# A gated MLP kernel: w_out in float16 parts, and transposes by VectorE and DRAM in place of TensorE's

## The chip, the cores and the metric

The kernel runs on one core of one Trainium2 chip. A core has five engines, each with its own instruction queue and strict order: TensorE (PE; its weight loads are shown apart as PEld), VectorE (DVE), ScalarE (ACT), GpSimd (POOL) and SyncE (SP), which here issues nearly all DMAs. The metric is the device time of one execution in microseconds (us).

## The reference

x has 2048 rows of 512. A softmax attention with 32 heads of 16 comes first, then a gated MLP whose gate mixes rows:

```
h  = x + attention(LN(x) @ wqkv) @ wo
z  = gelu(LN(h) @ w_in)               # 2048 x 1376
z1, z2 = z[:, :688], LN(z[:, 688:])
g  = w_sp @ z2 + b_sp                 # w_sp is 2048 x 2048
h2 = h + (z1 * g) @ w_out             # w_out is 688 x 512
```

Both LN are without weights. All is float32.

## The kernel before

Matrix products with near-float32 results are made of two float16 parts (high and low, the low part being the rest after the high): `mm3` issues three matmuls for one (high x high, high x low, low x high; lines 108 to 110), and `split` makes the parts (99 the high part on ACT, 105 the low one on VectorE). The program has these stages, on one core:

- **Up to about 165 us:** LN(x) and the projection to q, k, v.
- **To about 1295 us: attention.** PE, VectorE and ACT are nearly full; POOL works through a list of chores with durations that a planner spreads over the loop, among them the scaling and splitting of w_sp, w_in, wo, and of w_out in six pieces (`out_piece`), which go to DRAM as float32-like pairs (`wu_scr`).
- **1296 to 1455 us, "the middle".** Sixteen blocks of 128 rows in the order 0, 1, 8, 9, 2, 10, 3, 11, ..., 7, 15. Step k works on several blocks at once: 12 matmuls of width 512 make h of block k+2 (`make_h`, L743) from o's parts (`split_o`, ACT's high part L735 and VectorE's low part L736), VectorE adds x (L747) and takes the statistics, nb (L764) is the LN's shift, ACT normalises to hn (L1274). `turn` transposes hn on PE in four 128x128 steps (L1191), and `split` makes hT's parts. z of block k comes in four groups of 12 matmuls (`make_z`), the right half first; ACT takes the gelu (L1206). VectorE's statistics zst (L1268) and zmv (L1219) of z's right half lead to another nb (L764, also a helper's line, now from zmv); ACT normalises z (L1222); z's left half goes to DRAM (`z_scr`).
- From k with a partner (rows 8 on), `gate_z` makes the parts of the gate's seven products from both blocks' z: b22, b21, b11 and t1, t2, t3, n4 (a scheme with seven products in place of eight). `parts` writes the high part (L1210) on ACT or POOL and the low one (L1211) on POOL or VectorE. `meanwhile` asks for the next operand block of w_sp, multiplies o by its factors on POOL (L730), and asks for o, rc and xr of a block further on (L722, L725, L728 on SP).
- **1456 to 1731 us, "the end".** Eight pairs p of row blocks (p, p+8). A pair is seven products (`product`, 24 matmuls of width 344 each) into PSUM tiles A, B, C; between them ACT and VectorE build pr = z1 * g for both blocks (p1 L1397, q5, v; VectorE's L1412, L1416, L1420, L1426). `Out` transposes pr on PE in float32 (six steps of 128, L1327), splits it into fp32r parts, multiplies by w_out's pairs `wu` in 17 matmuls of 512 (mm3, L1352, L1353), and adds h (L1357). The transposes and the output of one pair stand between the products of the next.

`manual_schedule` means that in the middle and the end each engine's order is the order in which the code is written. Tiles live in pools; the pools of the middle are released as wholes, and the first DMAs into the end's tiles wait for that.

Of the kernel before, what the change touches and what calls it, by code (L numbers as in the profile page):

```python
# [40 lines left out]
FB = [(i * P, min(P, FH - i * P)) for i in range(6)]  # L41
# [18 lines left out]
def block_kernel(ctx: ExitStack, tc: tile.TileContext, x, wqkv, wo, w_in, w_sp4, b_sp, w_out, out):  # L60
# [30 lines left out]
    wu_scr = [dram.tile([P, 2, D], F32, name=f"wu{i}_scr") for i in range(len(FB))]  # L91
# [625 lines left out]
    def load_o(sb):  # L717

        c = slice(sb * P, (sb + 1) * P)
        o = e2.tile([P, DB, P], F32, name="o")  # L720
        for d in range(DB):
            nc.sync.dma_start(o[:, d, :], o_scr[d, :, :DH, c])  # L722
        rc = e2.tile([P, DB, P], F32, name="rc")
        for d in range(DB):
            nc.sync.dma_start(rc[:, d, :], r_scr[8 * d:8 * d + 8, c].rearrange(  # L725
                "h (o s) -> h o s", o=1).to_broadcast([8, DH, P]))
# [5 lines left out]
    def split_o(sb):  # L732
        o = os_.pop(sb)
        o2s[sb] = [e2.tile([P, DB, P], F16, name=f"o2{i}", bufs=1) for i in range(2)]
        nc.scalar.activation(o2s[sb][0], o, AF.Copy, scale=o_up)  # L735
# [48 lines left out]
    with ExitStack() as at:  # L784
# [181 lines left out]
        def out_piece(i):  # L966

            f0, n = FB[i]
            got, load = piece(w_out[f0:f0 + n, :], n)
            t = []  # L970

            def high():
                t.append(wp.tile([P, 2, D], F32R, name="wup", bufs=4)[:n])
                pool.tensor_copy(t[0][:, 0], got[0])

            def low():
                pool.tensor_sub(t[0][:, 1], got[0], t[0][:, 0].bitcast(F32))

            job(load, [(lambda: times(got[0], out_down), TS), (high, CAST), (low, TT)], 12)
            soon(len(chores) + LATER, lambda: nc.sync.dma_start(wu_scr[i][:n], t[0].bitcast(F32)))  # L980

# [69 lines left out]
        for i in range(len(FB)):  # L1051
            out_piece(i)
# [6 lines left out]
        for n in range(0, len(units), 2):  # L1059
# [86 lines left out]
            if n in (476, 480, 504, 508):  # L1146
                asked.append(load_o(h_rows[{476: 0, 480: 1, 504: 2, 508: 3}[n]]))
            if n in (484, 488, 508):
                asked.pop(0)()
            if n in (488, 500, 510):  # L1150
                split_o(h_rows[(n - 488) // 11])
# [28 lines left out]
    with ExitStack() as mid:  # L1180
# [13 lines left out]

        def new_z(sb):
# [13 lines left out]
        def parts(name, k, src, eh, el):  # L1209
            (nc.gpsimd.tensor_copy if eh == "pool" else nc.scalar.copy)(T[name][0][:, k, :], src)  # L1210
            (nc.gpsimd if el == "pool" else nc.vector).tensor_sub(T[name][1][:, k, :], src, T[name][0][:, k, :])  # L1211

        def gate_z(sb, meanwhile):
# [30 lines left out]
            e.tensor_sub(t2, b21, t2)  # L1244
            parts("n4", k, t2, eh, el)

        row = dict(enumerate(h_rows))
        with tc.manual_schedule(engines={E.PE, E.Activation, E.DVE, E.Pool, E.SP}):
# [3 lines left out]
            for k in range(NB):  # L1252
# [4 lines left out]
                if k + 3 < NB:  # L1257
                    split_o(row[k + 3])
                if new is not None:
                    mv, rs = scale_h(new)  # L1260
                    nb = minus_mean(e2, mv, rs)
                new_z(sb)
                make_z(sb, 1, 0)
                if k + 1 < NB:
                    turn(row[k + 1])
                make_z(sb, 1, 1)
                for c in range(2):
                    nc.vector.bn_stats(zst[sb][:, c, :], zs[sb][1][:, c * FC:(c + 1) * FC])  # L1268
                make_z(sb, 0, 0)
                make_z(sb, 0, 1)  # L1270
                hTs.pop(sb)
                if new is not None:
                    hns[new] = e2.tile([P, D], F32, name="hn", bufs=3)
                    nc.scalar.activation(hns[new], xrs.pop(new), AF.Identity, bias=nb, scale=rs)  # L1274
# [5 lines left out]
                def meanwhile():  # L1280
                    if k + 4 < NB:
                        asked.pop(0)()
                    if k + 5 < NB:
                        asked.append(load_o(row[k + 5]))
# [6 lines left out]
    with ExitStack() as fin:  # L1291
# [4 lines left out]
        ps_g = fin.enter_context(tc.tile_pool(name="fin_g", bufs=4, space=PSUM))  # L1296
        WB = len(FB) - 1
        TW = P // 2
        fn = FB[-1][1]
# [9 lines left out]
        class Out:  # L1309


            def __init__(self, tb, h, pr):
                self.rows, self.h, self.pr = slice(tb * P, (tb + 1) * P), h, pr
                self.pT = self.acc = None

            def turn(self, *halves):

                if self.pT is None:
                    self.pT = [f2.tile([P, WB + 1, P], F32R, name="pT0"),
                               f2.tile([P, WB, P], F32R, name="pT1")]  # L1320
                    self.tps = {}
                for half in halves:
                    i0 = 3 * half
                    tp = self.tps[half] = ps_t.tile([P, 4, P], F32, name="tp")
                    for i in range(i0, i0 + 3):
                        c = i * P if i < WB else FH - TW
                        nc.tensor.transpose(tp[:, i - i0, :], self.pr[:, c:c + P], ident)  # L1327

            def split(self, *halves):

                hi, lo = self.pT
                for half in halves:
                    i0, tp = 3 * half, self.tps.pop(half)
                    n = 3 - half
                    nc.scalar.activation(hi[:, i0:i0 + 3, :], tp[:, :3, :], AF.Copy)  # L1335
                    nc.vector.tensor_sub(lo[:, i0:i0 + n, :], tp[:, :n, :], hi[:, i0:i0 + n, :].bitcast(F32))
                    if half:
                        t = hi[TW:, WB, :]
# [127 lines left out]
```

## Time and profile before

| | us |
|---|---|
| median of 3 executions (1732.65 to 1733.68) | 1732.87 |
| the profiled execution | 1732.66 |
| its span, first to last instruction | 1730.9 |
| PE busy / DVE / ACT / POOL | 1713.6 / 1389.4 / 1301.3 / 824.8 |
| granted TensorE clock | 1.000 |

A row of the time line reads: start, duration, engine, line, operation, output <- input, shape, and in brackets how long the engine stood idle before it and what released it. A row of a group reads: line, engine, operation, names, count | busy us, mean ns | idle us before them and the releasers. A row of a table by windows reads: from:to, length, busy us of PE, PEld, DVE, ACT, POOL with their instruction counts, granted clock, share of the DMA engines, GB/s. A matmul's end in the profile is modelled, so the pace of matmuls is read from their starts.

### The profile page before, as it was taken

How to read it: one execution, taken by the hardware profiler on the slowest of the kernel's cores; microseconds unless marked ns; L12 is line 12 of the kernel's file. 1: busy time of each engine (PE TensorE's matmuls, PEld its weight loads, DVE VectorE, ACT ScalarE, POOL GpSimd, SP SyncE). 2: the span in 40 equal slices, each digit the busy share in tenths (PEclk: the TensorE clock that was granted, in tenths of full speed). 3: DMA queues.
4: the chain of work that ended last, by engine and by line, in shares of the span. 5: the costliest groups of instructions: out<-in, count | busy, mean ns of one | idle time of the engine just before them, and what ended most of it. 6: DMA issues, size and time to landing. Idle time of an engine off the chain costs nothing.

```text
span 1730.9 us, 36558 instructions
## 1 busy us (share of the span) xinstructions
PE 1713.6 (99%) x13581; PEld 676.1 (39%) x13581; DVE 1389.4 (80%) x2896; ACT 1301.3 (75%) x2566; POOL 824.8 (48%) x1088
## 2 busy tenths in 40 slices
PE   9999999999999999999999999999999999999999
PEld 4433222222222222222222222222226666777776
DVE  7688999999999999999999999999927776111112
ACT  4334999999999999999999999999995554011000
POOL 1231867776672267877677767600004665100110
PEclk9999999999999999999999999999999999999999
DMA  5534332342231244445345434410125454743440
GB/s 183 162 97 143 101 88 74 98 100 73 75 71 29 63 124 134 139 125 150 92 141 139 133 111 128 108 23 9 45 58 143 131 172 149 274 148 132 171 173 25
DMA packets 185482, 196.13 MB, mean 113 GB/s; under 512 B 65960, under 2 KB 134632, under 8 KB 185304
## 3 DMA queue, kind: packets, MB, share of 16 engines
q1 hardware_dynamic: 183000, 188.16, 37.0%
q10 hardware_dynamic: 2304, 5.64, 0.9%
q8 instruction: 106, 1.74, 0.4%
q14 instruction: 72, 0.59, 0.1%
HBM read 124.92 MB, written 68.75 MB: 112 GB/s over the span
## 4 chain that ended last, share of the span: by engine, by line
PE 72%; DVE 15%; POOL 4%; ACT 3%; DMA 2%; issue 2%; SPq 1%; ACTq 0%; POOLq 0%; DVEq 0%
PE pv L826 24%; PE s L801 16%; PE m L224 9%; DVE mx L229 7%; PE g L108 4%; PE g L110 4%; PE g L109 4%; PE acc L108 3%; PE acc L110 3%; PE acc L109 3%; DMA rc<-r_scr 2%; DVE ab L238 1%; POOL op L1003 1%; ACT pt L810 1%; DVE og L836 1%
## 5 line engine op out<-in xcount | busy, mean ns | idle before, releaser
L810 ACT ACTIVATE pt<-s 128x512 f32<-128x512 f32 x1968 | 1006.9, 638 | 4.7 <-PE m L224 3.6
L229 DVE TENSOR_REDUCE mx<-m 128x1 f32<-128x512 f32 x1510 | 947.2, 682 | 12.8 <-PE m L224 3.9
L801 PE MATMUL s<-qst,kst 50*128 50x512 f16 x2048 | 604.4, 379 | 0.4
L826 PE MATMUL pv<-pt,vst 128*32 128x256 f32 (+1 forms) x6056 | 598.1, 466 | 4.1 <-DVE og L836 0.7
L224 PE MATMUL m<-kst,qst 48*128 48x512 f16 x1510 | 452.3, 381 | 0.0
L801 PEld LDWEIGHTS <-kst 50*128 50x128 f16 x2048 | 131.9, 94 | 352.1 <-issue 322.7
L826 PEld LDWEIGHTS pv<-pt,vst 128*32 128x32 f32 x6056 | 119.5, 108 | 289.9 <-issue 276.6
L224 PEld LDWEIGHTS <-qst 48*128 48x128 f16 x2048 | 159.3, 93 | 173.7 <-issue 123.8
L224 PE MATMUL m<-uvs,qst 48*128 48x512 f16 x504 | 190.7, 380 | 0.0
L238 DVE CUSTOM_DVE_ANT_0 ab<-m,ab 128x512 f32<-128x512 f32 x252 | 170.3, 676 | 2.7 <-ACT ab L234 2.7
L234 ACT ACTIVATE ab<-m 128x512 f32<-128x512 f32 x252 | 157.7, 626 | 16.5 <-PE m L224 15.8
L246 POOL TENSOR_SCALAR nm<-nm 128x16 f32<-128x16 f32 x32 | 6.5, 204 | 331.4 <-DVE nm L243 331.4
L1335 ACT ACTIVATE pT<-tp 128x384 fp32r<-128x384 f32 x32 | 14.0, 488 | 142.0 <-PE tp L1327 142.0
L1413 POOL TENSOR_TENSOR pr<-pr,z 128x344 f32<-128x344 f32 x8 | 7.3, 910 | 193.1 <-DVE pr L1412 181.7
L1003 POOL TENSOR_TENSOR op<-raw,op 128x512 f16<-128x512 f32 x80 | 92.8, 1160 | 5.8
L910 POOL TENSOR_TENSOR raw<-raw 128x512 f32<-128x512 f32 (+1 forms) x84 | 83.1, 989 | 6.7
L915 POOL TENSOR_TENSOR acc_sp<-acc_sp,raw 128x512 f32<-128x512 f32 x63 | 80.4, 1276 | 4.5
L110 PE MATMUL acc<-wi,hT 128*128 128x344 f16 x256 | 79.2, 309 | 2.1 <-DVE hT L105 2.1
L1357 DVE TENSOR_TENSOR y<-acc,h 128x512 f32<-128x512 f32 x16 | 11.1, 691 | 85.9 <-PE acc L1353 84.5
L108 PE MATMUL acc<-wi,hT 128*128 128x344 f16 x256 | 79.1, 309 | 0.0
L109 PE MATMUL acc<-wi,hT 128*128 128x344 f16 x256 | 79.1, 309 | 0.0
L907 POOL TENSOR_SCALAR raw<-raw 128x512 f32<-128x512 f32 (+1 forms) x88 | 52.1, 592 | 19.7 <-DMA raw<-in_wqkv 12.4
(227 smaller groups left out, 2269.3 us busy)
## 6 DMA issues: line engine op xcount, KB each, us to landing
raw<-in_w_sp SPq DMA_DIRECT2D x128, 256.0 KB
s_scr<-op SPq DMA_DIRECT2D x64, 256.0 KB
op<-s_scr SPq DMA_DIRECT2D x32, 512.0 KB
a_scr<-op SPq DMA_DIRECT2D x48, 256.0 KB
op<-a_scr SPq DMA_DIRECT2D x24, 512.0 KB
o_scr<-og SPq DMA_DIRECT2D x64, 128.0 KB
qst<-q_scr SPq DMA_DIRECT2D x192, 32.0 KB
kst<-k_scr SPq DMA_DIRECT2D x48, 128.0 KB
```

Of the source, the lines that this page charges most:

```text
L108: nc.tensor.matmul(ps, lh, rh, start=first, stop=False, **kw)
L109: nc.tensor.matmul(ps, lh, rl, start=False, stop=False, **kw)
L110: nc.tensor.matmul(ps, ll, rh, start=False, stop=last, **kw)
L224: nc.tensor.matmul(acc, q[r, p, c], keys[r, p], start=True, stop=True)
L229: nc.vector.reduce_max(at(t, e if t else e - 1), acc, axis=AX.X)
L234: nc.scalar.activation(ab[0], acc, AF.Abs)
L238: nc.vector.tensor_tensor_reduce(ab[0], acc, ab[0], 0.5, LOW, ALU.add, ALU.max, at(0, 0))
L801: nc.tensor.matmul(s, kst[hg % 2][r, p, kb * P:(kb + 1) * P], qst[hg * NQ + qb][r, p, :], start=True, stop=True)
L810: nc.scalar.activation(pts[p, kb][:, t, :], s, AF.Exp, scale=scales_[hg // 2])
L826: nc.tensor.matmul(pv[0][32 * j:32 * j + 32, a:b], vst[hg % 2][:, c:c + 32], pts[j % 2, kb][:, j // 2, a:b], start=kb == 0, stop=kb == NB - 1,
L910: pool.tensor_mul(got[0] if n else acc, got[0], got[0])
L1003: chores.append((lambda: pool.tensor_sub(t[0][:, 1], of(), t[0][:, 0]), TT))
```

## The change

Three things change.

**w_out in float16 parts, made late.** The six chores on POOL and `wu_scr` go. At the start of the end w_out is fetched raw (`raw_w`, one DMA of five blocks and two small ones), VectorE takes the largest magnitude of each row (`weigh_w`, six reduces), a small matmul against ones spreads it (`measure_w`, ahead of product b22 of the first pair), and ACT and VectorE scale and split six blocks into float16 parts.

**The output projection.** Rows of pr are first scaled by a power of two (`level` on VectorE, `raise_` on ACT). The transposition is VectorE's 32x32 squares, sent to DRAM (`t_scr`) and brought back so that the squares land as whole 128x128 transposes (`squares`, `send`, `bring`); ACT takes the high part, VectorE the low part, in float16. The two halves of pr's columns go separately, each with its own accumulator, and `gather` (VectorE) scales and adds them to h. All of it belongs to the pair before. For the last pair PE transposes stay (`turn`).

**LN(h) for z.** hn is transposed the same way (`squares`, `bring`, `join`; `hn_scr` in DRAM), except for rows 0 and 1 of the order. ACT makes hn earlier, right behind the gelu of z's right half; the join for block k+1 stands in step k.

Beside these, the low part of b21 is put off to the next step, the last block's b22, b21 and n4 are made on POOL alone, the last asks for o in attention move by a few steps with o's high part on VectorE there, and the PSUM pool of the products is cut into two of two tiles.

In the middle, VectorE's and ACT's rows between two nb's in a step with a partner (nb from mv is LN(h)'s, zst and zmv belong to z, `whole` is what came back from DRAM). VectorE before and after:

```order
L764 TENSOR_SCALAR nb<-rs_u,mv 128x1
L105 TENSOR_TENSOR hT_21594<-tp,hT_21593 128x512
L1268 BN_STATS zst<-z_21572 128x6 x2
L1219 BN_AGGR zmv<-zst 128x2
L115 TENSOR_SCALAR rs_v_21646<-zmv 128x1
```

```order
L769 TENSOR_SCALAR nb<-rs_u,mv 128x1
L1285 BN_STATS zst<-z_21532 128x6 x2
L106 TENSOR_TENSOR hT_21585<-whole,hT_21584 128x512
L1185 STREAM_TRANSPOSE squares<-hn 128x4x4x32
L1231 BN_AGGR zmv<-zst 128x2
L116 TENSOR_SCALAR rs_v_21622<-zmv 128x1
```

The low part of hT has moved behind z's statistics and reads SBUF in place of PSUM, and the squares stand between it and the aggregate. ACT in the same step, before and after:

```order
L735 ACTIVATE o_21549<-o,fig_1850 128x512
L1206 ACTIVATE z_21572<-acc,fig_1847 128x344
L99 ACTIVATE hT_21593<-tp 128x512
L1206 ACTIVATE z_21572<-acc,fig_1847 128x344
L1206 ACTIVATE z_21571<-acc,fig_1847 128x344 x2
L1274 ACTIVATE hn<-xr,nb,rs_u 128x512
```

```order
L738 ACTIVATE o_21527<-o,fig_1850 128x512
L1212 ACTIVATE z_21532<-acc,fig_1847 128x344 x2
L1283 ACTIVATE hn<-xr,nb,rs_u 128x512
L100 ACTIVATE hT_21584<-whole 128x512
L1212 ACTIVATE z_21531<-acc,fig_1847 128x344 x2
L1229 DMA z_scr<-z_21531 128x688
```

The high part of hT stood between the two gelus of z's right half, ahead of hn; now it stands behind hn.

On SP, one step of the middle from one write of h to the next, before and after:

```order
L748 DMA h_scr<-xr 128x512
L722 DMA o<-o_scr 128x1x128 x4
L725 DMA rc<-r_scr 128x1x128 x4
L728 DMA xr<-in_x 128x512
L748 DMA h_scr<-xr 128x512
```

```order
L753 DMA h_scr<-xr 128x512
L1186 DMA hn_scr<-squares 128x512
L723 DMA o<-o_scr 128x1x128 x4
L1193 DMA whole<-hn_scr 32x4x128 x4
L727 DMA rc<-r_scr 128x1x128 x4
L730 DMA xr<-in_x 128x512
L753 DMA h_scr<-xr 128x512
```

A write and four reads are added, with the asks for o between them. On PE, the seam between products t2 and b22 of the first pair of the end (tp and w are measure_w's), before and after:

```order
L109 MATMUL g<-t_1_20721,op 128x344
L110 LDWEIGHTS op
L110 MATMUL g<-t_0_20720,op 128x344
L108 LDWEIGHTS op
L108 MATMUL g<-b_0_20716,op 128x344
L109 LDWEIGHTS op
```

```order
L111 MATMUL g<-t_0_20678,op 128x344
L1352 MATMUL tp<-w_23112,every 128x6
L109 LDWEIGHTS op
L109 MATMUL g<-b_0_20674,op 128x344
L110 LDWEIGHTS op
L110 MATMUL g<-b_1_20675,op 128x344
```

The measuring matmul now stands ahead of b22 and needs all six of VectorE's reduces.

The diff, cut to its core:

```diff
 def load_o(sb, between=lambda: None):
...
+    between()
...
-        def out_piece(i):
...
-        for i in range(len(FB)):
-            out_piece(i)
...
+        def squares(sb):
+            t = m2.tile([P, 4, DB, 32], F32, name="squares")
+            nc.vector.transpose(t.rearrange("p q d a -> p d q a"), hns.pop(sb))
+            nc.sync.dma_start(hn_scr[k % 2], t.rearrange("p q d a -> p (q d a)"))
+
+        def bring(sb):
+            hTs[sb] = t = m2.tile([P, 4, DB, 32], F32, name="whole")
+            src = hn_scr[k % 2].rearrange("(j b) (q c) -> q b j c", j=4, q=4)
+            for q in range(4):
+                nc.sync.dma_start(t[32 * q:32 * q + 32].rearrange("b j d a -> b j (d a)"), src[q])
+
+        def join(sb):
+            src = hTs[sb].rearrange("p j d a -> p d j a")
+            hTs[sb] = [m2.tile([P, DB, P], F16, name=f"hT{i}") for i in range(2)]
+            split(*[t.rearrange("p d (j a) -> p d j a", a=32) for t in hTs[sb]], src, "act")
...
-            parts("b22", k, b22, "act", el)
+            parts("b22", k, b22, "pool" if last else "act", "pool")
...
-            parts("b21", k, b21, "act", None)
+            parts("b21", k, b21, "pool" if last else "act", "pool" if last else "later")
...
+                new_z(sb)
+                make_z(sb, 1, 0)
+                if not k:
+                    turn(row[1])
+                if subs:
+                    subs.pop()(nc.vector)
                 if new is not None:
                     mv, rs = scale_h(new)
                     nb = minus_mean(e2, mv, rs)
-                new_z(sb)
-                make_z(sb, 1, 0)
-                if k + 1 < NB:
-                    turn(row[k + 1])
                 make_z(sb, 1, 1)
+                if new is not None:
+                    hns[new] = e2.tile([P, D], F32, name="hn", bufs=3)
+                    nc.scalar.activation(hns[new], xrs.pop(new), AF.Identity, bias=nb, scale=rs)
...
+                if k and k + 1 < NB:
+                    join(row[k + 1])
                 make_z(sb, 0, 0)
                 make_z(sb, 0, 1)
...
+                    squares(new)
...
                 product(C, "t1")
...
                 if p:
-                    before[1].turn(0, 1)
-                    before[1].split(0, 1)
+                    before.bring(0)
+                    before.hi(1)
+                    before.lo(1)
+                    before.lower(1, 0, 1)
+                    accs = [before.multiply(1, w) for w in range(2)]
+                else:
+                    weigh_w()
                 product(A, "t2", False)
...
+                else:
+                    measure_w()
                 product(C, "b22", False)
...
+                    before.hi(0)
+                    before.lo(0)
+                    before.lower(0, 0, 1)
+                    accs = [before.multiply(0, w) for w in range(2)]
                 product(A, "t3", False)
...
+                now.level(1, 0, 1)
+                now.raise_(1, 0, 1)
...
+                if not last:
+                    now.squares(1)
                 product(B, "b21")
...
+                    now.send(1)
...
                 product(A, "n4", False)
+                if not last:
+                    now.bring(1)
```

More of the change, by code (lines that the diff above doesn't have):

```diff
@@ L964, in split_piece @@
             job(load, steps, 12)
-        def out_piece(i):
[L968 to L980, printed above, removed]
         def quarters(p, c):
@@ L1307, in product @@
             ask()
[L1309 to L1338, printed above, removed]
-                        nc.vector.tensor_sub(t, tp[TW:, n, :], t.bitcast(F32))
-            def multiply(self, blocks, end=True):
-                first = self.acc is None
-                if first:
-                    self.acc = ps_o.tile([P, 512], F32, name="acc")
-                hi, lo = self.pT
-                for i in blocks:
-                    a, z = first and i == blocks[0], end and i == blocks[-1]
-                    if i < WB:
-                        mm3(self.acc, hi[:, i, :], lo[:, i, :], wu[:, i, 0, :], wu[:, i, 1, :], a, z)
-                    else:
-                        nc.tensor.matmul(self.acc, hi[:, i, :], wu5[0], start=a, stop=False)
-                        nc.tensor.matmul(self.acc, hi[:, i, :], wu5[1], start=False, stop=z)
-            def store(self):
-                y = f2.tile([P, D], F32, name="y")
-                nc.vector.tensor_add(y, self.acc, self.h)
-                nc.sync.dma_start(out[self.rows, :], y)
```

255 lines of the change are left out of this document (199 added, 56 removed).

## The prediction, made before the changed kernel ran

> **What bounds the kernel now.** I read the page's busy lines first, then a table by stage, then the waits and the order of time inside two of the stages. The stages below are the middle (1296 to 1455 us: h, LN(h), z, gelu and the gate's operands, 16 blocks of rows) and the end (1456 to 1731 us: eight pairs of row blocks, each seven spatial products and an output projection).
>
> ```profile
> PE 1713.6 (99%) x13581; PEld 676.1 (39%) x13581; DVE 1389.4 (80%) x2896; ACT 1301.3 (75%) x2566; POOL 824.8 (48%) x1088
> 1362.50:1404.10 41.60, 40.87 (x259) 25.10 (x257) 33.36 (x107) 21.63 (x38) 27.86 (x32) 1.00 0.52 154
> 1465.00:1472.00 7.00, 7.00 (x50) 4.70 (x48) 0.52 (x1) 0.55 (x1) 0.20 (x1) 1.00 1.01 375
> 1586.00:1619.50 33.50, 33.50 (x214) 23.79 (x213) 5.88 (x12) 3.27 (x7) 3.20 (x5) 1.00 0.45 163
> ```
>
> PE looks full everywhere, but the stages differ. In the end it is full in truth (33.50 of 33.50, DVE 5.88, ACT 3.27). In the middle 40.87 of 41.60 hides that matmul ends are modelled, and the waits say more:
>
> ```profile
> L110 PE MATMUL acc<-wi,hT 128*128 128x344 f16 x240 | 74.2, 309 | 2.1 <-DVE hT L105 2.1
> L1222 ACT ACTIVATE z<-z,nb,rs_u 128x688 f32<-128x688 f32 x15 | 14.4, 961 | 42.5 <-DVE nb L764 38.0 <-DMA o<-o_scr 4.5
> L1274 ACT ACTIVATE hn<-xr,nb,rs_u 128x512 f32<-128x512 f32 x14 | 11.3, 811 | 14.1 <-DVE nb L764 14.1
> L1211 DVE TENSOR_TENSOR b<-z,b 128x344 f16<-128x344 f32 x7 | 3.6, 517 | 15.5 <-ACT b L1210 15.5
> L736 DVE SCALAR_TENSOR_TENSOR o<-o,fig,o 128x512 f16<-128x512 f32 x12 | 12.5, 1044 | 4.8 <-ACT o L735 3.3 <-DMA rc<-r_scr 1.6
> ```
>
> ACT waits for VectorE's nb and VectorE for ACT's b and o: a loop through two engines in strict order, while neither is full, and PE waits for its product hT. The loop in order of time, one block of rows:
>
> ```profile
> 1379.37 0.21 DVE L764 TENSOR_SCALAR nb<-rs_u,mv 128x1 f32<-128x1 f32 x1
> 1379.50 0.68 DVE L105 TENSOR_TENSOR hT<-tp,hT 128x512 f16<-128x512 f32 x1
> 1379.62 0.81 ACT L1274 ACTIVATE hn<-xr,nb,rs_u 128x512 f32<-128x512 f32 x1 [0.83 <-DVE nb L764]
> 1380.10 0.93 DVE L1268 BATCH_NORM_STATS2 zst<-z 128x6 f32<-128x344 f32 x2
> 1381.06 0.21 DVE L1219 BATCH_NORM_AGGREGATE zmv<-zst 128x2 f32<-128x12 f32 x1
> 1383.36 0.21 DVE L764 TENSOR_SCALAR nb<-rs_u,zmv 128x1 f32<-128x1 f32 x1
> 1383.61 0.96 ACT L1222 ACTIVATE z<-z,nb,rs_u 128x688 f32<-128x688 f32 x1 [3.18 <-DVE nb L764]
> 1384.60 0.86 ACT L1210 CAST b<-z 128x344 f16<-128x344 f32 x2
> 1385.37 0.72 ACT L735 ACTIVATE o<-o,fig 128x512 f16<-128x512 f32 x1
> 1385.49 0.52 DVE L1211 TENSOR_TENSOR b<-z,b 128x344 f16<-128x344 f32 x1 [1.92 <-ACT b L1210]
> 1394.76 0.21 DVE L764 TENSOR_SCALAR nb<-rs_u,zmv 128x1 f32<-128x1 f32 x1
> 1404.11 0.21 DVE L764 TENSOR_SCALAR nb<-rs_u,zmv 128x1 f32<-128x1 f32 x1
> ```
>
> The z-side nb comes at 1383.36, 1394.76, 1404.11: a block with a partner ready ("heavy", rows from 8 on) takes 11.40, the other ("light") 9.35, a pair 20.75, 10.38 a block. PE's own work is less:
>
> ```profile
> 1378.04 2.75 PE L743 MATMUL acc<-wo,o 128*128 128x512 f16 x12
> 1380.63 0.31 PE L108 MATMUL acc<-wi,hT 128*128 128x344 f16 x1
> 1382.38 0.60 PE L1191 MATMUL tp<-ident,hn 128*128 128x128 f32 x4
> 1382.82 0.31 PE L108 MATMUL acc<-wi,hT 128*128 128x344 f16 x1
> 1582.65 0.82 PE L1327 MATMUL tp<-ident,pr 128*128 128x128 f32 x6
> 1583.31 0.31 PE L108 MATMUL g<-b,op 128*128 128x344 f16 x1
> 1586.69 0.51 PE L108 MATMUL acc<-wu,pT 128*128 128x512 f32 x1
> 1590.78 0.32 PE L108 MATMUL g<-t,op 128*128 128x344 f16 x1
> ```
>
> Starts give the prices: 12 f16 matmuls of 512 take 2.59 (1378.04 to 1380.63; 0.2155 each), four transposes 0.44 (1382.38 to 1382.82), six 0.66 (1582.65 to 1583.31), a product of 24 matmuls 3.50 (t2 at 1463.85 to b22 at 1467.35, shown further down), and 17 output matmuls 3.97 (the product from 1583.31 ends at 1586.81; the next starts at 1590.78). A middle block is 2.59 + 48 x 0.146 (7.0) + 0.44 = 10.03 on PE.
>
> **The parts.** The sum is made against the profiled execution, 1732.7 (span 1730.9 and 1.8 around it), 0.2 under the median.
>
> *End, PE.* A pair takes 7 x 3.504 + 2 x 3.97 + 2 x 0.655 = 33.78 before. After: the same products and 34 f16 matmuls at 0.2155 = 7.33, no transposes: 31.86. Seven times -1.92 = **-13.4**. The new VectorE work (levels, squares, low parts, about 8 us a pair from rows of 0.5 to 1.0) lies beside 33.5 with 5.88 used, ACT's likewise. The road of half 1 (level, raise, squares, a write, four reads, hi, lo) lies between product t3 of one pair and product t1 of the next: I make that 13.3 of the 14.0 us there are (four products) if the write lands 2.4 and the reads 3.5 behind their issue (estimates, under the 5.9 that 1.2 MB take in the rows below); 0.7 to spare. In the first pair VectorE's six low parts of w_out (about 1.0 each, L736's mean) stand ahead of the gate: +1.4. The last pair keeps PE transposes, now behind a level and a raise: +1.2, and its shorter matmuls give -0.8. End in all **-11.7** (-13.4 to +4).
>
> *Start of the end.* This is what the trace shows there:
>
> ```profile
> 1456.56 0.21 DVE L764 TENSOR_SCALAR nb<-rs_u,zmv 128x1 f32<-128x1 f32 x1
> 1463.56 0.79 SPq L1368 DMA_DIRECT2D z<-z_scr  x2
> 1463.85 0.31 PE L108 MATMUL g<-t,op 128*128 128x344 f16 x1 [0.56 <-ACT p L1397]
> 1464.40 0.90 SPq L1368 DMA_DIRECT2D h<-h_scr  x2
> 1465.35 3.60 SPq L1380 DMA_DIRECT2D wu<-wu_scr  x5
> 1467.35 0.31 PE L108 MATMUL g<-b,op 128*128 128x344 f16 x1
> 1471.20 0.52 DVE L1412 TENSOR_TENSOR pr<-g,v 128x344 f32<-128x344 f32 x1 [8.11 <-DMA wu<-wu_scr]
> L1211 POOL TENSOR_TENSOR b<-z,b 128x344 f16<-128x344 f32 x15 | 12.6, 837 | 17.7 <-ACT b L1210 17.7
> L229 DVE TENSOR_REDUCE mx<-m 128x1 f32<-128x512 f32 x1510 | 947.2, 682 | 12.8 <-PE m L224 3.9
> ```
>
> The pools of the middle come free when the last operand part is done; SP's first fetch, 7.0 behind the last nb, waits for that, and so does ACT's p1, for which PE's t2 waits. b22 starts 10.8 behind nb (1467.35). After: those last parts stand on POOL in one chain of ten (casts about 0.5, the rest 0.84 to 0.91), starting when ACT's norm ends at nb + 1.2: free at nb + 8.6. Then SP asks for z and h (1.2 MB) and raw_w (1.4 MB); at the 375 GB/s that this stretch shows, 2.6 MB take 7.0, and with 0.5 ahead of SP's first issue and some 2.8 for the issues and the way there raw_w is in at nb + 18.9. VectorE's six reduces, 0.6 to 0.68 each, end at nb + 22.6, and PE stands at the measuring matmul ahead of b22 until then. b22 at nb + 22.9: **+12.1** (+8 to +16). In before wu had until the second pair, so nobody waited for it. Part of b11 is done earlier, in the middle's holes, which gains nothing here, since PE waits anyhow.
>
> *Middle.* PE loses 0.44 a block and its wait for hT. But the loop gets longer. Between the h-side nb and the z-side aggregate stood L105 and the two statistics: 1379.37 to 1381.06, 1.69. Now VectorE's low part of hT waits for ACT's hi, which stands behind hn: 0.25 + 0.81 + 0.72 (L735, the nearest row to a cast from SBUF) = nb + 1.8; then the low part (between L105's 0.68 and, with both inputs in SBUF, L736's 1.04; taken 0.9) and the squares (not in the trace; between a statistics pass over 512, half of 0.93 x 512/344 = 0.69, and L736's 1.04; taken 0.7, with one input like the former): aggregate at nb + 3.2, +1.5 a block, 1.0 to 2.1. VectorE's wait of 1.92 for b goes (the low part is done a block later): -0.75 a pair, since ACT's o is late next. Pair 20.75 + 3.0 - 0.75 = 23.0, 11.5 a block: +1.1 in 12 blocks = **+13.5** (0 to +20). Behind hi on ACT stand the gelus of z's left half, so a late whole also holds PE's accumulators. SP gets five more issues a block, and behind the four reads, which wait for the write to land, stand rc and xr of a block that is due only three blocks on. The issues:
>
> ```profile
> 1388.62 2.48 SPq L722 DMA_DIRECT2D o<-o_scr  x4
> 1391.14 2.43 SPq L725 DMA_DIRECT2D rc<-r_scr  x4
> ```
>
> The write's issue (about 0.4, of one like xr's), o's four between, and four reads like o's are 5.4 with nothing for landing. The far end: z and h above, 1.2 MB, are used 7.6 behind their first issue, 5.9 behind their last; two such landings make 14.6. One block is 256 KB, so I stand nearer to the low end: 8 to 10. With hi, lo and squares behind it (2.3) a turn is some 11, just under the loop's 11.5; its own ends are 7.7 and 16.9.
>
> *Attention.* The six chores of w_out leave POOL, and two high parts of o move from ACT to VectorE: 0. POOL, 48% busy, bounds nothing there.
>
> Sum: 13.5 + 12.1 - 11.7 = +13.9, so 1732.7 + 13.9 = 1746.6.
>
> **Two rules against the rows.** The Trainium skill (VectorE: DVE Perf Modes, section "The three transpose paths") has 390 ns for a 128x128 transpose on TensorE against 311 on VectorE, and advises TensorE where PSUM will do. By its 390 the 140 transposes that leave PE would be worth 55 us, an estimate; the rows above (0.109 each in a run) make them 15, and the sum stays with the rows. The Trainium skill (TensorE: Matmul & The Clock Gate, section "HAM oscillation — how this bites in real kernels") warns that a PE gap over about 3.4 us halves the clock for a while; no row of before has a gap so long or a granted clock under 1.00. My start of the end has a gap of about ten: by that rule the next 3.4 us run at half speed, an estimate of +1.7, and the time would be 1748.3.
>
> **Rivals.**
> - *The middle becomes PE-bound, and the change is faster (0.14).* If joining and squares fit into VectorE's holes (8.2 of 41.6 us idle in the table), blocks fall to PE's 9.6: 13 x -0.8 = -10; with +12.1 and -11.7 about 1723. For it: the idle time and the 15.5 us of waits for b; against: VectorE and ACT work in strict order, and the new wait stands between their nb's. It decides where the aggregate comes under 1.7 + 0.4 = 2.1 behind the h-side nb, which gives the loop 10.4 a block.
> - *The way by DRAM binds the middle (0.12).* At 12.5 a block, 12 x 2.1 = +25 in place of +13.5: about 1758. For it: nine issues in a row on one queue between write and use; against: 9.2 of the loop's 11.5 are there to hide them, and transfers ran at 154 GB/s there where 375 is shown.
> - *Half 1 comes late in every pair (0.10).* 1.3 x 6 = +8: about 1754.
> - *raw_w is there early (0.08).* The stall shrinks by 8: about 1738, still slower.
>
> The forecast itself has 0.56. The range leaves out the faster rival and the top of the second: 1731 to 1758. Faster by over 0.2% (3.5 us, about what a measurement of this kernel can tell from no change): 0.15; within it 0.04, from the low ends of the middle's term; slower 0.81.
>
> **What would show it.** Z-side nb's 11 to 12 us apart in the middle, VectorE idle at the low part of hT with ACT's hi as releaser, PE waiting for hT or o in every block. A gap on PE of 8 to 12 us behind t2, ended by VectorE's reduce, with raw_w in front. Pairs of 31.9 us with no wait at the output matmuls. Wrong if blocks stay at or under 10.4 us, if that gap is under 4 us, or if pairs take over 33 us.

## The result, and the profile after

The changed kernel takes 1787.42 us (median of 4, 1785.24 to 1788.46) against 1732.99 before (4 runs): 1.031 times, 95% interval 1.0298 to 1.0322. It is slower, as forecast, but by 54 us, not by 14; 1787 lies far outside the stated 1731 to 1758.

The page's first part and the row of granted clock, changed kernel:

```profile
PE 1717.6 (96%) x13443; PEld 640.1 (36%) x13443; DVE 1458.9 (82%) x3065; ACT 1320.2 (74%) x2584; POOL 816.5 (46%) x1062
PEclk9999999999999999999999999999998998999999
```

PE has 138 matmuls fewer and is busy 4 us longer. One reason for the latter shows in the second row: two of its 40 digits are 8, so TensorE runs below its full clock in places. Two tables by windows, cut at the same events of both kernels: first to last z-side nb (the middle), to the start of b22, b22 itself, the rest. First the kernel before (b22 stands at the end of its second row), then the changed one. The windows stand up to 0.3 us beside the events; the differences in the table under them are between the events themselves:

```profile
1308.50:1456.80 148.30, 145.40 (x929) 90.88 (x928) 114.88 (x372) 77.26 (x136) 97.23 (x116) 1.00 0.47 146
1456.80:1470.90 14.10, 13.54 (x94) 8.96 (x93) 4.13 (x6) 4.21 (x8) 2.39 (x3) 1.00 0.52 185
1470.90:1730.90 260.00, 256.22 (x1617) 182.28 (x1615) 47.52 (x97) 24.78 (x53) 24.71 (x39) 1.00 0.43 154
```

```profile
1308.50:1481.90 173.40, 153.19 (x892) 88.41 (x891) 123.76 (x383) 78.50 (x136) 99.32 (x114) 0.94 0.55 165
1481.90:1505.50 23.60, 8.50 (x48) 5.08 (x46) 4.98 (x8) 2.97 (x5) 7.31 (x10) 0.76 0.63 211
1505.50:1511.90 6.40, 6.40 (x26) 3.44 (x27) 4.81 (x11) 3.78 (x6) 0.52 (x1) 0.54 0.56 224
1511.90:1786.50 274.60, 249.27 (x1533) 148.65 (x1531) 99.23 (x236) 41.48 (x71) 23.58 (x24) 0.99 0.52 167
```

| | forecast | measured |
|---|---|---|
| up to the middle | 0 | -0.3 |
| middle, first to last z-side nb | +13.5 | +25.4 |
| last nb to the start of b22 (10.8 to 23.8) | +12.1 | +13.0 |
| b22 itself (3.5 to 6.4, at clock 0.54) | 0 | +2.9 |
| the rest of the end | -11.7 | +14.6 |
| sum | +13.9 | +55.6 (the profiled spans) |

So one term came out as worked, the middle's was half of what it is, and the one that should have paid for both has the wrong sign.

**The middle.** The chain of waits of the changed kernel, one turn (start, duration, what):

```profile
1417.08 0.62 DVE squares L1185
1417.73 5.93 DMA hn_scr<-squares
1423.73 0.33 SPq L1193
1424.10 0.43 SPq L1193
1424.57 0.43 SPq L1193
1425.04 2.67 DMA whole<-hn_scr
1427.82 0.64 ACT hT L100
1428.48 1.17 DVE hT L106
1429.65 0.62 DVE squares L1185
```

From squares to squares 12.57 us, and nothing of PE in it. The write needs 5.93 until it has landed; only then may SP issue the reads. This turn is one of the shorter ones: in the ten turns from 1328 to 1444 the reads are issued 5.6 to 7.6 behind the write, and the z-side nb's from 1344.24 to 1458.85 come to 12.7 a block. The waits of the middle (engine, line, what for: us, times, longest) show who pays:

```profile
POOL o L732 <- DMA rc<-r_scr: 52.7, 9, 8.5
PEld L109 <- ACT hT L100: 19.4, 9, 3.5
ACT hT L100 <- DMA whole<-hn_scr: 5.9, 6, 1.7
```

PE's weight loads wait 19.4 us for hT's high part, ACT waits for the reads, and POOL for rc, which SP asks for behind the reads.

**The start of the end**, from the time line of the changed kernel:

```profile
1491.34 0.45 PE L109 MATMUL g<-t,op 128*128 128x344 f16 x1 [6.49 <-ACT p L1517]
1501.30 3.65 DVE L1346 TENSOR_REDUCE w<-raw_w 128x1 f32<-128x512 f32 x6 [16.45 <-DMA raw_w<-in_w_out]
1505.06 0.56 PE L1352 MATMUL tp<-w,every 128*128 128x6 f32 x2 [8.61 <-issue]
```

The release, raw_w's arrival, the end of the six reduces and the start of b22 come 0.4 to 0.9 us later behind the last nb than the prediction had them.

**A pair of the end**, the time line of the shortest of the changed kernel's seven (34.70 us from product n4 to the next n4): half 1's write and reads, and what PE's two waits hang on.

```profile
1520.46 0.32 SPq L1409 DMA_DIRECT2D t_scr<-squares  x1
1523.01 1.75 SPq L1417 DMA_DIRECT2D whole<-t_scr  x4
1529.56 0.55 ACT L1519 ACTIVATE q<-g,fig 128x344 f32<-128x344 f32 x1 [2.95 <-PE g L111]
1530.00 0.83 ACT L1423 ACTIVATE pT<-whole 128x768 f16<-128x768 f32 x1
1530.89 0.39 PE L109 MATMUL acc<-wu,pT 128*128 128x512 f16 x1 [1.37 <-ACT pT L1423]
1541.65 0.52 DVE L1536 TENSOR_TENSOR pr<-g,v 128x344 f32<-128x344 f32 x1 [6.32 <-PE g L111]
1542.09 0.95 DVE L1432 TENSOR_TENSOR pT<-whole,pT 128x768 f16<-128x768 f32 x1
1543.09 0.39 PE L111 MATMUL acc<-wu,pT 128*128 128x512 f16 x1 [1.11 <-DVE pT L1432]
```

PE waits twice in a pair, and here no transfer is in either wait. Half 1's reads are issued 2.55 us behind its write. Its high part (L1423) waits for no DMA: it follows q5 (L1519) at once, but q5 reads product t1 and so can't start before t1 is over. The output matmuls stand directly behind t1 on PE, so PE waits for q5 and the high part. In the same way half 0's low part (L1432) stands on VectorE behind the add of product b22 (L1536). By the starts of the matmuls the two waits cost 2.86 us (34.70 against 31.84 where they are absent, run 8 below), and no pair of the changed kernel is shorter than this one.

Late transfers come on top of that. Two pairs later:

```profile
1602.42 0.38 SPq L1409 DMA_DIRECT2D t_scr<-squares  x1
1609.68 1.74 SPq L1417 DMA_DIRECT2D whole<-t_scr  x4
1613.35 0.84 ACT L1423 ACTIVATE pT<-whole 128x768 f16<-128x768 f32 x1 [2.17 <-DMA whole<-t_scr]
```

Half 0's squares are ready at 1599.42, but their write is issued at 1602.42: ahead of it on SP stand half 1's reads, the next pair's z and h, and an operand. The reads are issued 7.3 us later (1609.68), and half 0's high part waits 2.17 for them. Pairs take 34.7 to 37.7 us, not 31.9. Over the seven pairs that is 27 us more than at run 8's pace; 7 x 2.86 = 20 of it are the two waits behind ACT's and VectorE's order, some 3.4 a lower clock in the two pairs of 37.7 and 37.2 (shown at the end), and the rest, some 4, late transfers.

### The profile page after: what moved, and what is told of

It is laid out like the page before. It is cut to its first block, busy times and chain, and to the rows that moved or that the text cites. A ratio compares the mean times of both kernels' runs of the same rounds, so it can differ in the third digit from the quotient of the medians.

```text
span 1786.5 us, 36673 instructions
## 1 busy us (share of the span) xinstructions
PE 1717.6 (96%) x13443; PEld 640.1 (36%) x13443; DVE 1458.9 (82%) x3065; ACT 1320.2 (74%) x2584; POOL 816.5 (46%) x1062
## 4 chain that ended last, share of the span: by engine, by line
PE 68%; DVE 13%; DMA 9%; POOL 3%; issue 2%; SPq 2%; ACT 2%; ACTq 0%; DVEq 0%; POOLq 0%
PE pv L831 24%; PE s L806 16%; PE m L225 9%; DVE mx L230 7%; DMA hn_scr<-squares 3%; PE acc L111 3%; PE acc L109 3%; PE acc L110 3%; PE g L109 3%; PE g L111 3%; PE g L110 3%; DMA whole<-hn_scr 2%; DMA t_scr<-squares 1%; DVE ab L239 1%; DVE og L841 1%
## 5 line engine op out<-in xcount | busy, mean ns | idle before, releaser
L1386 ACT ACTIVATE pr<-pr,up 128x304 f32<-128x304 f32 (+1 forms) x32 | 17.0, 574 | 137.2 <-DVE up L1340 137.2
L109 PE MATMUL acc<-wi,hT 128*128 128x344 f16 x256 | 83.3, 325 | 15.0 <-ACT hT L100 15.0
L111 PE MATMUL acc<-wi,hT 128*128 128x344 f16 x256 | 83.3, 325 | 4.3 <-DVE hT L106 4.2
L110 PE MATMUL acc<-wi,hT 128*128 128x344 f16 x256 | 83.2, 325 | 0.0
L732 POOL TENSOR_TENSOR o<-o,rc 128x512 f32<-128x512 f32 x16 | 20.3, 1270 | 124.5 <-DMA rc<-r_scr 56.4
L109 PE MATMUL g<-t,op 128*128 128x344 f16 x192 | 60.0, 313 | 6.5 <-ACT p L1517 6.5
```

The lines of the kernel that those rows point to most:

```text
L109: nc.tensor.matmul(ps, lh, rh, start=first, stop=False, **kw)
L110: nc.tensor.matmul(ps, lh, rl, start=False, stop=False, **kw)
L111: nc.tensor.matmul(ps, ll, rh, start=False, stop=last, **kw)
```

## The experiments

The theory after the result: a way by DRAM costs two landings and not some fixed small time, these landings stand in a queue with everything else, and each in-order wait on SP holds what is behind it. The rival is the prediction's own: the loop of VectorE and ACT, longer by order. For the end, the changed kernel's time line above shows a second rival, for which no run was made: ACT's and VectorE's order in a pair. Each time below is of one execution unless said otherwise; executions of the changed kernel lie up to 3.2 us apart, and the kernel before took 1732.6 to 1733.9 beside them.

**1. Middle's transposes back on PE.**

```diff
-                if not k:
-                    turn(row[1])
+                if k + 1 < NB:
+                    turn(row[k + 1])
...
-                    join(row[k + 1])
...
-                    squares(new)
+                    hns[new] = ...; nc.scalar.activation(hns[new], ...)
```

> The middle alone is put back: hn is transposed on PE, in the order of the kernel before; the end stays as changed. If all that the middle lost (last z-side nb at 1481.7 in place of 1456.6) comes from the new way of hT, the last nb stands at 1456 to 1458 and the time is 25 us under the changed kernel's, about 1762. If the other edits in the middle (b21's low part a step later, the last parts on POOL) cost part of it, the last nb stays above 1460 and the time above 1766.

Measured: 1755.34, span 1753.6; last z-side nb at 1453.1. All of the middle's loss is the new way of hT with the order that goes with it. The last nb is even 3.4 earlier than in the kernel before: VectorE's wait of 1.92 for b in every second block is gone (b21's low part is made a step later), which the prediction had at 0.75 a pair and which shows as blocks of 10.74 and 9.35 against 11.40 and 9.35 before. The rest of the end loses 4 us less than in the changed kernel: its pairs take 34.7 to 36.0 at a clock of 1.00, and the two pairs at a lower clock are not there.

**2. The way by DRAM cut out of the loop.**

```diff
+        fixed = m2.tile([P, 4, DB, 32], F32, name="fixed", bufs=1)
+        nc.gpsimd.memset(fixed, 0.25)
 def join(sb):
-            src = hTs[sb].rearrange("p j d a -> p d j a")
+            src = fixed.rearrange("p j d a -> p d j a")
```

> The changed kernel, but hT's parts are made from a constant tile instead of the block that came back from DRAM (hT is then not LN(h)); squares, write and reads are all still made. The way by DRAM is thus no longer in the loop, while the orders of VectorE and ACT and the traffic stay. If the way by DRAM alone binds the middle, blocks fall to PE's or the old loop's 9.6 to 10.4, the last nb to 1450 to 1457, the time by 25 to 30. If the loop of VectorE and ACT that the prediction forecast lies just under it, blocks come to 11.5, the last nb to 1469 to 1471, the time by 11 to 13. If neither binds (rc's lateness behind the reads), nothing falls.

Measured: 1782.22; last nb at 1478.6, only 3.1 earlier. Neither the way by DRAM alone nor the engines' loop foretold that; it is nearest to the third case named, rc's lateness behind the reads. The chain of waits, shares by line from 1310 to 1450, says why:

```profile
by line: DMA hn_scr<-squares 23.0%; DMA rc<-r_scr 17.1%; issue 5.9%; DMA o<-o_scr 5.8%; DVE hT L106 5.6%; SPq L1193 5.4%; DMA whole<-hn_scr 5.1%; SPq L727 4.6%; DVE rs_t L126 3.4%; DVE squares L1185 3.1%; ACT hT L100 3.1%; POOL o L732 2.7%;
```

The write's landing is still in it, now by another way: SP holds the reads until the write has landed, rc stands behind the reads, POOL multiplies o by rc, ACT and VectorE split o, and VectorE's LN(h) stands behind that. Two loops went through one landing, and they are nearly equally long: with the squares' way out of the loop the blocks hardly fall.

**3. No write and no reads at all.**

```diff
-            nc.sync.dma_start(hn_scr[k % 2], t.rearrange("p q d a -> p (q d a)"))
...
-            for q in range(4):
-                nc.sync.dma_start(t[32 * q:32 * q + 32]..., src[q])
```

(with the constant tile of run 2)

> As the run with the constant tile, and the write and the four reads are left out too (squares are still made; hT is not LN(h)). That run gained 3 us in the middle, not 11. If what held it was rc, which stands behind the reads on SP, and these behind the landing of the write, that chain is gone too, and the loop of VectorE and ACT is left: 11.5 a block by the prediction, last nb at 1469 to 1471. If the engines' loop is shorter than forecast, blocks come to 10 to 10.5 and the last nb to 1453 to 1458. If it stays at 1477 or more, the engines' own orders bind and not the DMAs.

Measured: 1773.29. From the time line, VectorE's nb's:

```profile
1405.27 0.21 DVE L769 TENSOR_SCALAR nb<-rs_u,mv 128x1 f32<-128x1 f32 x1
1408.12 0.17 DVE L1230 BATCH_NORM_AGGREGATE zmv<-zst 128x2 f32<-128x12 f32 x1
1410.38 0.21 DVE L769 TENSOR_SCALAR nb<-rs_u,zmv 128x1 f32<-128x1 f32 x1
1422.25 0.21 DVE L769 TENSOR_SCALAR nb<-rs_u,zmv 128x1 f32<-128x1 f32 x1
```

This is the loop that the prediction worked out, by itself: 11.87 for the heavy block shown, 10.46 for a light one (1399.91 to 1410.38, 1422.25 to 1432.71), 11.17 a block against a forecast of 11.5; the aggregate comes 2.85 behind the h-side nb (forecast 3.2). Around it VectorE waits for ACT alone (0.56 for hT's high part, 0.78 to 1.16 for o's). Last nb 1465.7: +9.2 against before, where +13.5 was forecast. rc's loads still have 22.7% of this run's chain of waits, but run 4, which has none of them, shows the same blocks of 11.86 and 10.47, so these are the engines' own. The loop exists, and is not what binds the changed kernel.

**4. rc out of the queues.**

```diff
-        rc = e2.tile([P, DB, P], F32, name="rc")
-        for d in range(DB): nc.sync.dma_start(rc[:, d, :], r_scr...)
+        rc = kept[0]        # the middle's blocks; loaded once
```

(shortened: the first five blocks still load theirs)

> The changed kernel without the loads of rc in the middle (one block's factors serve for all, so o is scaled wrongly); it takes 44 loads of 64 KB out of the queues. If the write lands 5.5 to 7.5 us behind its issue because of what is in the queues, it lands in 3 to 5 and blocks fall toward 11.2, last nb 1466 to 1472. If the landing is the way to DRAM itself, it stays over 5 us and the last nb at 1476 or later.

Measured: 1772.87, last nb 1466.6. The squares go by DRAM here as in the changed kernel, and yet most blocks are at the engines' loop (10.5 to 11.9). SP's queue in the time line:

```profile
1406.34 0.32 SPq L1192 DMA_DIRECT2D hn_scr<-squares  x1
1406.71 0.45 SPq L1170 DMA_DIRECT2D op<-s_scr  x1
1407.26 2.47 SPq L725 DMA_DIRECT2D o<-o_scr  x4
1409.83 1.82 SPq L1199 DMA_DIRECT2D whole<-hn_scr  x4
```

The reads start 3.5 us behind the write, as soon as o's issues are through, so the write has landed by then; in the changed kernel's turn above it took 5.93. In seven of the nine turns from 1327 to 1419 the reads start 3.0 to 3.5 behind the write. In one they start 5.1 behind it because SP's other issues last that long, and in one 5.0 behind it, 1.6 of it waiting. The way to DRAM has no fixed long landing: it is long where rc's four loads of 64 KB go ahead of it. Without them the transfers of xr and h lie further ahead of the write too (h's 2.7 to 6.1 us, in the changed kernel 0.2 to 1.4), so this run does not say how much is rc's share alone. rc's own chain (run 2) is gone here too, so it does not part the two chains either.

**5. The reads behind rc and xr.**

```diff
-        between()
         rc = e2.tile(...)
...
         nc.sync.dma_start(xrs[sb], x[c, :])
+        between()
```

> The changed kernel, with the four reads of the squares asked for behind rc and xr on SP instead of ahead of them. rc no longer waits for the write's landing. If that chain (write, its landing, reads, rc, POOL, o, nb) sets the blocks, they fall toward 11.2, last nb 1466 to 1472. If the squares' own way (write, landing, reads, hT, squares) sets them, the reads come up to 1 us later and the last nb stays at 1479 to 1490.

Measured: 1811.11, blocks of 14 to 15.5, last nb 1505.5. The squares' own way sets the blocks, by more than was written. Part of its chain:

```profile
1396.70 0.57 SPq L726
...
1399.67 0.43 SPq L1193
1400.15 1.17 SPq L1193
1401.36 0.43 SPq L1193
1401.83 4.17 DMA whole<-hn_scr
1406.03 0.64 ACT hT L100
```

The write is no longer in the chain. The reads are: they stand behind rc and xr on SP and their last now needs 4.17 to land, against 2.67 above. So what comes behind rc's loads lands late: the write in the changed kernel, the reads here. Freeing rc alone gains nothing. But this run makes the squares' way longer, so it can't tell which of the two nearly equal chains ends last in the changed kernel; that is read from the changed kernel's own chain of waits from 1310 to 1450, in which the landing of the squares' write has 40.3% and rc's loads 4.1%.

**6. From SBUF to SBUF.**

```diff
-            nc.sync.dma_start(hn_scr[k % 2], ...)
...
+            for j in range(4):
+                for q in range(4):
+                    nc.sync.dma_start(t[32 * q:32 * q + 32, j], src[32 * j:32 * j + 32, q])
```

> The changed kernel with the squares sent straight from one SBUF tile to the other in sixteen DMAs of 32 partitions, so that no write to DRAM has to land ahead of the reads. If that landing (5.5 to 7.5 us) is what binds, the way is one landing long, 3 to 5 us behind 5 us of issues: blocks of 11.5, last nb at 1469 to 1472. If SP's sixteen issues (0.33 to 0.43 each) take over, blocks stay at 12.5 or more.

Measured: 1875.96, blocks of some 19. One row of SP's time line:

```profile
1403.40 11.66 SPq L1196 DMA_DIRECT2D whole<-squares  x16
```

Sixteen issues take 11.66 us, 0.73 each with the waits between them, where 0.33 to 0.43 was expected. With rc's loads (2.6), o's (1.9 to 4.1), xr and h behind them SP has hardly a gap left in a block: SP is the bound. That a single landing would do is left open: it was never on its own here.

**7. The measuring matmul later.**

```diff
-                else:
-                    measure_w()
                 product(C, "b22", False)
...
                 product(B, "b21")
+                if not p:
+                    measure_w()
```

> The changed kernel, with the measuring matmul and what follows it behind product b21 of the first pair in place of ahead of b22. If PE's stall ahead of b22 is the wait for raw_w and the six reduces alone, b22 follows t2 at once: the 8.9 us gap goes and so does the half clock over b22 (2.9 us), and 10 to 12 us are gained; t2 keeps its half clock, since the gap ahead of it stays. If the stall is bound by z and h too, it moves to the next wait (n4, which needs VectorE's add behind the reduces) and under 6 us are gained.

Measured: 1781.40; the span is 1779.6, 6.9 less than the changed kernel's, where 10 to 12 were expected. b22 does follow t2 at once and at full clock (the gap of 8.6 and the 2.9 are gone), but the next wait takes a part back:

```profile
1523.20 0.61 PE L109 MATMUL acc<-wu,pT 128*128 128x512 f16 x1 [4.35 <-ACT pT L1423]
```

The second pair's first output matmul waits 4.35 for ACT, at a low clock behind it (0.61 in place of 0.39).

**8. Output matmuls one product later** (with the late measuring).

```diff
-                    accs = [before.multiply(1, w) for w in range(2)]
...
                 product(A, "t2", False)
+                if p:
+                    accs = [before.multiply(1, w) for w in range(2)]
```

(and half 0's likewise behind t3; VectorE's sums of half 1 move behind b22 with them, and half 1's squares ahead of the sums of half 0)

> As the run with the late measuring matmul, and in each pair the output matmuls of half 1 stand one product later (behind t2, not t1), those of half 0 too (behind t3, not b22). If the pairs' extra 3 to 5 us are halves that come back from DRAM 1.7 to 2.5 and 1 to 3 us too late, one product (3.5 us) covers both: pairs of 31.9 to 32.3, 7 x 3.7 = some 25 us less than the run it is compared with, and no granted clock under 1.00 behind the first pair. If the lateness is bound by the DMA queue's own pace, it stays or moves and less than 10 us are gained.

Measured: 1754.78; the span of 1753.0 is 26.6 less than run 7's. One pair in a window:

```profile
1547.85:1579.69 31.84, 31.84 (x204) 19.77 (x202) 12.36 (x29) 5.32 (x9) 2.74 (x3) 1.00 0.68 219
```

31.84 us, full, clock 1.00, while DMA moves 219 GB/s: the pair that the prediction worked out (31.86), and five of the seven are so. One product of distance covers everything that PE waited for in a pair, late transfers and the order of ACT and VectorE alike, so this run does not part the two; the time line of a pair above does, and there the order is the larger share. The expectation read all of PE's wait as halves coming back late. The first pair is not covered: it takes 37.25, with PE waiting 3.58 for p1 (L1517), which stands on ACT behind the scaling of rows, and this behind w_out's six low parts on VectorE. The prediction had +1.4 for those parts.

**9. The end's transposes back on PE** (in the changed kernel).

```diff
-                    before.send(0)
...
+                    for w in range(2):
+                        before.turn(1, w); before.split(1, w)
```

> The changed kernel with the end's transposes put back on PE for every pair (12 a pair, levels, raises and float16 parts as changed; nothing goes by DRAM). If the way by DRAM is what holds the pairs at 34.7 to 37.7, they come to 24.53 + 7.33 + 1.31 = 33.2 with no wait, some 18 us under the changed kernel, 1768 to 1772. If it is the new work of ACT and VectorE, they stay over 34.5.

Measured: 1772.21; the span of 1770.4 is 16.1 less than the changed kernel's. A pair:

```profile
1556.98:1590.13 33.15, 33.15 (x216) 21.14 (x214) 10.54 (x26) 5.27 (x11) 3.08 (x5) 1.00 0.49 165
```

33.15 with no wait: so the new work of ACT and VectorE is not what holds the pairs. The run does not part the way by DRAM from the order, since it changes both: the parts of half 1 are made behind b11 and those of half 0 behind t1, a product or more ahead of the matmuls that use them. Float16 parts of w_out alone give 0.63 a pair, and the transposes by VectorE, where their use stands a product later (run 8), another 1.31.

**10. What the runs point to.** The middle on PE with b21's low part later, the last block's parts as before, the measuring matmul behind b21, w_out's low parts behind the first pair's work on VectorE, output matmuls a product later.

```diff
-            parts("b22", k, b22, "pool" if last else "act", "pool")
+            parts("b22", k, b22, "act", el)
...
+        def low_w():
+            for i in range(2 * 3):
+                nc.vector.scalar_tensor_tensor(wu[1][:, i, :], ...)
```

> The middle on PE as before with b21's low part a step later, the last block's parts spread over three engines as before, the measuring matmul behind b21, w_out's low parts behind the first pair's other work on VectorE, output matmuls a product later. The middle ends 3.4 us earlier than before (the run with PE's turns: last nb 1453.1), the start has before's stall of 2 us and no half clock, seven pairs at 31.85 (-13.4), the last pair +1: 1732.7 - 3.4 - 13.4 + 1 = 1717. If the first pair still waits for w_out's parts, up to 5 more.

Measured: 1719.25. The same kernel in five more executions:

> The best run once more, timed in rounds against the kernel before: 1719 to 1720, a ratio of 0.992.

1718.38 us (1717.68 to 1719.00, 5 runs) against 1733.12 (9 runs): 0.9915, interval 0.9902 to 0.9929: 0.85% faster than the kernel before, and so faster than both kernels. By windows, the middle and the rest of the end:

```profile
1308.20:1452.20 144.00, 144.00 (x933) 92.17 (x932) 115.19 (x370) 77.22 (x136) 97.68 (x115) 1.00 0.49 150
1466.40:1716.50 250.10, 243.22 (x1535) 150.03 (x1533) 106.94 (x253) 44.78 (x77) 21.02 (x25) 1.00 0.60 200
```

From the first to the last nb it is 144.1 in place of 148.0, and the rest of the end is 250.1 in place of 260.0. The end's -9.9 is -13.4 from PE less what the first and last pair wait.

**11. The same with the end's transposes on PE.** (Runs 9 and 10 together.)

> As the best run so far (1719.3), but with the end's transposes on PE in place of squares by way of DRAM. Twelve transposes a pair at 0.109 are 1.31, times seven 9.2: 1728 to 1730. If the squares' way costs something that this one saves (VectorE's squares, DMA traffic), 1722 to 1726.

Measured: 1733.59, 14 more than run 10, not 9. 9.2 of it are the transposes. The second pair's first transposes also wait:

```profile
1486.87 1.12 PE L1446 MATMUL tp<-ident,pr 128*128 128x128 f32 x4 [4.16 <-POOL pr L1441]
```

POOL's copy stands behind a memset that waits for w_out's low parts on VectorE, and product t1 behind this gap takes 5.6 for 3.5. So the way by DRAM for pr pays, once its use stands a product later.

## Why the prediction was wrong, point by point

- **The middle, +13.5.** The mechanism forecast is there (run 3: 11.17 a block, +9.2), but another binds. The prediction listed it as a rival, priced it at 12.5 a block and +25, and gave it 0.12; the trace shows 12.57 for a turn and +25.4. The step that failed is "I stand nearer to the low end: 8 to 10" for write and reads, and with it "a turn is some 11, just under the loop's 11.5": its own upper figure of 10, with the 2.3 behind it, already gives 12.3. From the write's issue to the reads' landing it is 10.0 in the turn shown (1417.73 to 1427.71), of which the write's landing takes 5.9, and the write's landing takes up to 7.6 in others. The landing was taken as a matter of the block's size; runs 4 and 5 show that it is a matter of what goes ahead in the queues. The far end of 14.6 had no measured landing behind it: the row from which "are used 7.6 behind their first issue" was read (L1412) is VectorE's add of b22 and v, which waits for PE's product and uses neither z nor h. That rc and xr behind the reads were "due only three blocks on" was wrong as well: run 2 shows rc's lateness to be a loop of its own, nearly as long.
- **The end, -11.7.** PE's price was right to 0.02 a pair (run 8). The step that failed is the overlap: "The road of half 1 (level, raise, squares, a write, four reads, hi, lo) lies between product t3 of one pair and product t1 of the next". It counts t1's time for hi and lo, but on ACT hi stands behind q5, and q5 needs the end of t1; so PE waits at least 1.37 in every pair, also in the one where the write landed 2.55 behind its issue, near the 2.4 assumed. Half 0, for which no road was worked out, costs nearly as much in the same way, behind VectorE's add of b22. Together these are 2.86 a pair, or 20 of the 26.3 us between forecast and measurement. The condition "if the write lands 2.4" failed too, in six of seven pairs (reads issued 4.7 to 5.8 behind half 1's write), but ACT's high part of half 1 waited for it visibly in one pair only, 0.64; whether it would cost more if hi stood earlier on ACT is not shown. The rival "half 1 comes late", with 1.3 a pair, has the size of half 1's wait but another cause.
- **The start, +12.1.** Right: +13.0, by the steps named (last parts on POOL, 2.6 MB of z, h and raw_w, six reduces).
- **The clock.** b22 took 6.4 for 3.5, at a granted clock of 0.54 behind a gap of 8.6. The trace agrees with the Trainium skill (TensorE: Matmul & The Clock Gate, section "HAM oscillation — how this bites in real kernels") that a gap over about 3.4 us lowers the clock. The estimate of +1.7 made from it was short by 1.2 for b22, and I had left it out of the sum since no row of before showed it. Product t2, behind the gap of 6.5, lost 1.4, which PE's next wait hides.
- **The transposes' worth.** 0.109 each by the rows is confirmed: run 9 against run 8 gives 1.31 for twelve.
- **The faster rival (PE-bound middle, 0.14)** needed the aggregate under 2.1 behind nb. Without any DMA it is 2.85 (run 3).
- **The range.** It left out what two listed rivals give together, as if only one could hold. But even both (25 in the middle, 8 in the end) come to 1732.7 + 25 + 12.1 - 11.7 + 8 = 1766. The way to 1787 is the end's order of ACT and VectorE, which no rival had.

## What to carry to other kernels

A road of write, landing, read, landing has to be priced by a transfer of like size in the same stage with the same neighbours in the queues, and every in-order issue queue that waits on a landing holds all that stands behind it. A conversion counts as hidden under a product only if nothing ahead of it on its own engine waits for that product's end: look at the order of the engine that makes the operand, and not only at the time it has. Work that leaves the busiest engine for such a road pays only where the use can be put a whole unit of work later: here one product (3.5 us) of distance, with the measuring matmul moved, turned the end's +14.6 into -7.0 (run 8: 253.0 from product t3 of the first pair on, 260.0 before), with no change to the work itself.

## What had not been expected of the hardware

- A 256 KB write landed 5.9 us behind its issue with rc's loads ahead of it, and within 3.5 in most turns without them (run 4).
- The clock was lower behind short gaps too. In one pair of the changed kernel PE's matmuls twice started 1.3 us apart (1.0 us idle each), with two matmuls between; the window behind them:

```profile
1579.00:1585.00 6.00, 5.90 (x22) 2.52 (x23) 0.29 (x3) 0.00 (x0) 0.00 (x0) 0.72 0.30 110
```

A mean clock of 0.72 there, and 1.7 us lost on sixteen matmuls (5.15 from 1579.10 on, 3.45 at 0.2155 each). The same is seen behind one gap of 2.2 us at 1673.92. It doesn't follow every such gap: the other pairs have waits of 1.4 and 1.1 us and a clock of 1.00, and what decides is not shown. The whole middle ran at 0.94, with no single wait of PE longer than 3.5 us.
- Sixteen small issues from SBUF to SBUF took SP 0.73 us each, waits included (run 6), against 0.44 for each of the four reads from DRAM (1.74 for four).
